# Long convolution and token MLP on one core: rows 0 and 1 of the last inverse step read four column blocks in place, with a new instruction order behind the last product

## The chip, the cores and the metric

The kernel runs on one core of one Trainium2 chip. The time is device microseconds of that core from launch to end. Each execution is one launch, and a time below is the median of several.

## The reference, cut to what matters

```python
# S = 2048 tokens, D = 448 channels, F = 1792
k_shift = sum(k_pad[:, t:t+S, :] * shift_k[:, 3-t] for t in range(4))     # short filter
kv = k_shift * v
y  = irfft(rfft(pad(kv, 2S)) * rfft(pad(ssm_k, 2S)))[:S]                  # long causal convolution
y  = y + kv * ssm_D
h  = x + layernorm(x) * y                                                 # x = A_q
u  = gelu(einsum("bsd,sf->bdf", layernorm(layernorm(h)), w1) + b1)        # MLP over tokens
h2 = h + transpose(einsum("bdf,fs->bds", u, w2) + b2)
```

## The kernel before, in words

The core has five queues: TensorE (PE in the profile), ScalarE (ACT), VectorE (DVE), GpSimd (POOL) and SyncE (SP, which only issues DMAs; POOL issues some too). One large SBUF tensor, "arena", holds everything, and PSUM has eight banks. The order of every queue is written out by hand in the table `ORDER`: a token `i2.1:0-3` means operations 0 to 3 of step 1 of stage `i2`. A small scheduler in the kernel reads this order, places the buffers and the semaphore waits; each engine then runs its list strictly in order.

The long convolution is done as matrix products with sine tables, two steps forward (`k1`, `u1`, then `k2`, `u2`) and two steps back (`i1`, `i2`). Tokens are numbered 16 q + r, so that "row r" (r = 0 to 15) is a tile of 128 tokens by 448 channels.

- Stage `i1` has eight products, jj = 0 to 7, and runs them in the order 0, 6, 3, 4, 5, 2, 1, 7. Their steps are `i1.1` (jj 0), `i1.14` (6), `i1.8` (3), `i1.10` (4), `i1.12` (5), `i1.6` (2), `i1.4` (1) and `i1.16` (7). For each, DVE multiplies the two transforms (L1161), PE applies the inverse table in two halves of eight matmuls (L1178), and ACT or DVE copies each half out of PSUM (the helper `evac`, L739 or L742) into `TU`. A product fills two column blocks of `TU`, j = 2 jj and 2 jj + 1.
- A block is then turned from "partitions are rows and frequencies" to "partitions are blocks and frequencies" by DMAs from `TU` into `TZ` (L1201; for the last product L1190). POOL issues most of the 196 KB ones, SP the small ones. Row r of `TZ` has a part from every block.
- Stage `i2` makes row r by two matmuls (L1300) of the table `ET` with row r of `TZ`. The row therefore waits for the DMAs of all blocks. For rows 0 and 1 (`NZ = 2`) the blocks 14 and 15 of the last product are left out of `TZ` (zeros are put there by two DMAs, L1119). Instead four more matmuls (L1308) multiply these blocks where they stand in `TU` with a table `EW` that is zero but for the partitions of that row. Four DMAs (L1128) copy the needed rows of `ET` into `EW`. The last product uses a rearranged inverse table, `ML`, so that rows 2 to 15 stand in its first 112 partitions and rows 0 and 1 in the last 16.
- `ct.0`, `ct.1` and `ct.2` are 24 transposes (L1109) that make the rest of `ET`. `warm` are 14 matmuls (L1211) whose result nobody reads; they keep PE busy at chosen places.
- After its matmuls a row is combined with x (DVE, L1338 for rows 0 to 3, L1327 for the others after a gate on ACT L1317 or DVE L1319). Its statistics are taken: bn_stats on DVE for rows 0 and 1 (L1344), a sum on DVE and a sum of squares on ACT (L1356) for the others, which go in pairs. POOL turns them into a scale (L1366, L1369, L1371, L1376, power at L1380). DVE normalises the row into `Q` (L1386). The steps of rows 0 to 8 are, on PE, `i2.1`/`i2.2` (row 0), `i2.9`/`i2.10` (row 1), `i2.17`, `i2.20`, `i2.28`, `i2.32`, `i2.41`, `i2.45` and `i2.54`.
- The MLP's first half keeps seven PSUM banks, one for each block of 128 hidden units, and adds row by row: `mlp.r` is seven matmuls with `Q[r]` (L1433). Only one bank is then left for the `i2` rows that follow, so these stand between the `mlp` steps. The second half of w1 (L1443) and w2 (L1454) come after it; they are PE work without a pause.
- Statistics of x itself (`q` steps: bn_stats L1237, aggregate L1239 on DVE, then add and power on POOL, L1245 and L1248) and the normalised rows 0 to 3 (`xn`, L1270 on ACT) run beside stages `i1` and `i2`.

The in-place matmuls of rows 0 and 1 follow the two of `TZ`:

```python
for h in range(2):                       # L1300
    matmul(bank, ET[:, 2*r+h, :], TZ[:, r, h, :], start=(h == 0), stop=(h == 1 and r >= NZ))
if r < NZ:
    for h in range(2):
        for jx in range(2):              # L1308, j = 14, 15
            matmul(bank, EW[:, 4*r+2*jx+h, :], TU[:, 14+jx, h, :], start=False, stop=(last))
```

Of the kernel before, what the change touches and what calls it, by code (L numbers as in the profile page):

```python
# [7 lines left out]
ALU = mybir.AluOpType  # L8
# [575 lines left out]
def _build(nc, A_q, A_k, A_v, A_shift_k, A_ssm_k, A_ssm_D, B_w1, B_b1, B_w2, B_b2, out):  # L584
# [5 lines left out]
    Bsz, S, D = A_q.shape  # L590
# [48 lines left out]
    with ctx:  # L639
# [48 lines left out]
        EW = view(o_EW, [4 * NZ, 128], f16)  # L688
        o_ML = o_EW + 1024 * NZ
# [414 lines left out]
        def emit_ct(late):  # L1104
# [10 lines left out]
            if not late:  # L1115
                sch.t0 = T_CT + 1.0
                for jx in range(2):
                    p0 = pz(R // 2 - 1, jx)
                    op("sp", lambda e, W, p0=p0: e.dma_start(  # L1119
                        TZ[p0:p0 + 29:4, 0:NZ].rearrange("p r c d -> p (r c d)"),  # L1120
                        EW[8 * jx:8 * jx + 8].rearrange("p a b -> p (a b)")[:, 0:NZ * D].bitcast(bf16)
                        .unsqueeze(1).broadcast_to([8, 2, NZ * D])),
                       r=[(o_EW, 1024 * NZ)], w=[(o_TZ, NZ * 2 * DB, "zpool")], dmab=8 * NZ * 2 * DB, keng=4, est=660.0)
                for r in range(NZ):
                    for jx in range(2):
                        p0 = pz(R // 2 - 1, jx)
                        q0 = 8 * (R - NZ) + r
                        op("sp", lambda e, W, r=r, jx=jx, p0=p0, q0=q0: e.dma_start(  # L1128
                            EW[q0:q0 + 7 * NZ + 1:NZ, 4 * r + 2 * jx:4 * r + 2 * jx + 2].rearrange("p a b -> p (a b)"),
                            ET[p0:p0 + 29:4, 2 * r:2 * r + 2].rearrange("p a b -> p (a b)")),  # L1130
                           r=[r_ET(r)], w=[(o_EW + 1024 * r + 512 * jx, 512)], dmab=8 * 512, keng=4, est=660.0)

        def emit_ew():
            sch.t0 = T_EW
            op("pool", lambda e, W: e.memset(EW, 0.0), w=[(o_EW, 1024 * NZ)], est=1100.0, safter=shuf["u"])
# [15 lines left out]
        def emit_products_i1():  # L1151
            for jj in range(R // 2):
# [20 lines left out]
                mt = (MA, MB, MN) if jj < R // 2 - 1 else ML  # L1173
                for h in range(2):
                    for t, (tab, xy) in enumerate(((mt[0], 0), (mt[2], 3), (mt[1], 1), (mt[1], 2))):
                        for par in range(2):
                            P = slice(64 * par, 64 * par + 64)
                            k = op("pe", lambda e, W, b=bs[h], m=ms[h], par=par, t=t, tab=tab, xy=xy, P=P: e.matmul(  # L1178
                                Pb(b, par), tab[P, :], MR(m.slots[0])[P, xy, :], start=(t == 0), stop=(t == 3)),
                               r=r_iv if jj < R // 2 - 1 else [(o_ML, 768)], br=[ms[h]], bw=[bs[h]], n=D, est=94.5, mode=3)  # L1180
                            i1_last.append(k)
                    evac(lambda jj=jj, h=h: TU[:, 2 * jj:2 * jj + 2, h, :], lambda b=bs[h]: Ppair(b),
                         [(o_TU + (4 * jj + h) * DB, DB), (o_TU + (4 * jj + 2 + h) * DB, DB)], bs[h], 2 * D)
                if jj == R // 2 - 1:
                    for h in range(2):
                        for par in range(2):
# [3 lines left out]
                            k = op("pool" if h and par == 0 else "sp", lambda e, W, j=j, h=h, p0=p0: e.dma_start(  # L1190
# [6 lines left out]
                for par in range(2):  # L1197
                    j = 2 * jj + par
                    p0 = 64 * (j & 1) + 32 * ((j >> 1) & 1) + (j >> 2)
                    for q_, a, b_, j0 in (("sp" if j == 3 else "pool", 0, 112, 0), ("pool" if jj == 2 else "sp", 112, 128, 14)):  # L1200
# [25 lines left out]
        def emit_q():  # L1226
# [4 lines left out]
            for g in range(8):  # L1231
# [9 lines left out]
                if g >= 2 and g % 2 == 0:  # L1241
                    continue
                r0, nr = (2 * g, 2) if g < 2 else (2 * g - 2, 4)
# [40 lines left out]
        def emit_i2():  # L1284
# [5 lines left out]
            for g, (r0, ng) in enumerate(GR):  # L1290
                oh = o_hst + 64 * g
                hs = view(oh, [16], f32)
                for i in range(ng):
# [4 lines left out]
                    tz = [(o_TZ + r * 2 * DB, 2 * DB)]  # L1298
                    for h in range(2):
                        k = op("pe", lambda e, W, b=b, r=r, h=h: e.matmul(  # L1300
                            Pb(b), ET[:, 2 * r + h, :], TZ[:, r, h, :], start=(h == 0), stop=(h == 1 and r >= NZ)),
                           r=[r_ET(r)] + tz, bw=[b], n=D, after=av[-1:] if r >= 8 and h == 0 else ())
                    if r < NZ:
                        sch.t0 += 0.2
                        for h in range(2):
                            for jx in range(2):
                                j = R - 2 + jx
                                k = op("pe", lambda e, W, b=b, r=r, h=h, j=j, jx=jx: e.matmul(  # L1308
                                    Pb(b), EW[:, 4 * r + 2 * jx + h, :], TU[:, j, h, :], start=False, stop=(h == 1 and jx == 1)),
                                   r=[(o_EW + 1024 * r + 512 * jx + 256 * h, 256), (o_TU + (2 * j + h) * DB, DB)], bw=[b], n=D, safter=(k,))  # L1310
# [41 lines left out]
                    else:  # L1352
# [4 lines left out]
                                                                             scale=1.0 / math.sqrt(D),  # L1357
# [5 lines left out]
                if ng == 2:  # L1363
# [6 lines left out]
                                                                   op=ALU.mult), r=[(oh + 16, 8)], w=[(oh + 24, 8)], est=290.0)  # L1370
                    op("pool", lambda e, W, hs=hs: e.tensor_tensor(out=hs[:, 8:10], in0=hs[:, 2:4], in1=hs[:, 6:8],  # L1371
# [145 lines left out]
```

## Time and profile before

| what | value |
|---|---|
| median of 3 runs | 173.05 us (172.36 to 174.24) |
| the profiled execution | 172.33 us, of which span 170.4 us |
| PE busy in the span | 161.8 us (95%), 1425 matmuls |
| DVE, ACT, POOL busy | 99.8, 92.3, 60.0 us |
| granted TensorE clock | 1.000 |
| last product of `i1` ends issuing on PE | 70.76 us |
| first MLP matmul (`mlp.0`) | 79.82 us |
| PE, DVE, ACT, POOL busy in the 9.06 us between | 8.28, 8.94, 8.20, 5.92 us |

The span is the time from the first to the last instruction; the profiled execution's own time is 1.9 us longer. A PE matmul of 448 columns is shown some 0.35 us long, but the next one starts 0.19 us after it: they overlap. Where the text counts PE work, it counts the distance between starts.

### The profile page before, as it was taken

The page shows a single profiled execution, that of the slowest core. Times are in us where ns is not written, and L with a number is a line of the kernel's source. Part 1 is how long each engine was busy: PE and PEld are TensorE (multiplying, and loading weights), DVE is VectorE, ACT ScalarE, POOL GpSimd, SP SyncE. Part 2 cuts the span into 40 slices and gives each one's busy share as a digit, 9 for nine tenths or more (in the row PEclk, how much of TensorE's full clock was granted, in tenths as well). Part 3 has the DMA queues.
Part 4 walks back from the last instruction along what each step waited for, and adds up shares of the span by engine and source line. Part 5 has one row for each costly group of instructions (what it writes and reads, how often), then busy time and mean ns, then how long its engine had stood idle before and what let it go on. Part 6 is the DMA issues. An engine that isn't in the chain of part 4 may idle for free.

```text
span 170.4 us, 3574 instructions
## 1 busy us (share of the span) xinstructions
PE 161.8 (95%) x1425; PEld 94.8 (56%) x1425; DVE 99.8 (59%) x188; ACT 92.3 (54%) x132; POOL 60.0 (35%) x154
## 2 busy tenths in 40 slices
PE   6989999889889999999999999999999999999993
PEld 2776745442334334553455555555567777777783
DVE  7998988859999999999969710000003223132232
ACT  3699588988999999979857518311210000000000
POOL 8345737581810686466887820000000000000000
PEclk9999999999999999999999999999999999999999
DMA  5999687584959766658999999950000111101111
GB/s 169 416 332 374 196 251 290 207 330 161 283 147 365 275 184 192 186 152 250 364 379 402 417 425 418 416 232 0 0 0 4 54 54 54 54 0 58 54 54 54
DMA packets 15612, 35.15 MB, mean 206 GB/s; under 512 B 3756, under 2 KB 9724, under 8 KB 15596
## 3 DMA queue, kind: packets, MB, share of 16 engines
q1 hardware_dynamic: 12540, 28.39, 45.6%
q0 software_dynamic: 2912, 6.45, 12.0%
q8 instruction: 11, 0.18, 0.4%
q10 hardware_dynamic: 144, 0.08, 0.2%
q14 instruction: 5, 0.04, 0.1%
HBM read 22.05 MB, written 1.84 MB: 140 GB/s over the span
## 4 chain that ended last, share of the span: by engine, by line
PE 57%; ACT 22%; DVE 11%; DMA 5%; POOL 2%; issue 1%; SPq 0%; DVEq 0%
PE ps L1454 25%; PE ps L1443 12%; PE ps L1433 12%; ACT arena L739 10%; ACT arena L1070 5%; DMA arena<-arena 5%; DVE arena L1161 5%; DVE arena L1237 4%; PE ps L1095 3%; ACT arena L848 2%; PE ps L1026 2%; PE ps L1300 2%; ACT arena L740 2%; POOL arena L1076 2%; ACT arena L1317 1%; PE ps L1060 1%
## 5 line engine op out<-in xcount | busy, mean ns | idle before, releaser
L1457 DVE SCALAR_TENSOR_TENSOR arena<-ps,arena 128x448 bf16<-128x448 f32 (+2 forms) x17 | 11.1, 656 | 57.7 <-PE ps L1454 57.6
L1454 PE MATMUL ps<-arena 128*128 128x448 bf16 (+2 forms) x238 | 42.7, 342 | 0.0
L1454 PEld LDWEIGHTS ps<-arena 128*128 128x128 bf16 x238 | 33.3, 145 | 9.5
L739 ACT CAST arena<-ps 128x896 bf16<-128x896 f32 x30 | 24.6, 1013 | 0.2 <-PE ps L1095 0.2
L1433 PE MATMUL ps<-arena 128*128 128x448 bf16 x112 | 22.5, 353 | 0.2 <-DVE arena L1376 0.2
L1070 ACT CAST arena<-ps 128x896 bf16<-128x896 f32 x24 | 20.5, 915 | 3.2 <-PE ps L1060 3.2
L1076 POOL DMA_DIRECT2D arena<-arena x32 | 17.6, 555 | 11.8 <-ACT arena L1070 9.8
L1443 PE MATMUL ps<-arena 128*128 128x448 bf16 x112 | 21.3, 352 | 0.0
L1423 ACT ACTIVATE arena<-ps,arena 128x448 bf16<-128x448 f32 x14 | 8.3, 635 | 19.1 <-PE ps L1443 14.6
L1095 PE MATMUL ps<-arena 128*64 128x448 bf16 x128 | 15.2, 359 | 2.3 <-ACT arena L739 0.8
L1161 DVE TENSOR_TENSOR arena<-arena 128x1792 bf16<-128x1792 bf16 x16 | 16.7, 1086 | 0.3 <-ACT arena L739 0.2
L1433 PEld LDWEIGHTS ps<-arena 128*128 128x128 bf16 x112 | 10.9, 98 | 10.7 <-DVE arena L1386 0.6
L1443 PEld LDWEIGHTS ps<-arena 128*128 128x128 bf16 x112 | 11.0, 98 | 10.2
L1060 PE MATMUL ps<-arena 128*32 128x448 bf16 x256 | 15.0, 355 | 0.8 <-DVE arena L1008 0.5
L1178 PE MATMUL ps<-arena 64*128 64x448 bf16 x128 | 14.5, 351 | 0.1
L1201 POOL DMA_DIRECT2D arena<-arena x15 | 8.8, 593 | 13.2 <-ACT arena L739 13.2
L1095 PEld LDWEIGHTS ps<-arena 128*64 128x64 f16 x128 | 5.8, 108 | 10.7 <-ACT arena L739 2.9
L1178 PEld LDWEIGHTS ps<-arena 64*128 64x128 f16 x128 | 6.1, 94 | 8.2 <-ACT arena L739 2.5
L1008 DVE TENSOR_TENSOR arena<-ps,arena 128x512 bf16<-128x512 f32 (+1 forms) x16 | 9.1, 618 | 2.0 <-PE ps L993 1.8
L739 ACT COPY arena<-ps 128x1024 bf16<-128x1024 bf16 (+1 forms) x8 | 8.0, 1064 | 3.1 <-PE ps L967 3.1
L1356 ACT ACTIVATE arena<-arena 128x448 bf16<-128x448 bf16 x14 | 8.0, 574 | 2.7 <-DVE arena L1327 2.6
L1060 PEld LDWEIGHTS ps<-arena 128*32 128x32 f16 x256 | 5.1, 95 | 7.6 <-DVE arena L1008 2.5
(97 smaller groups left out, 192.9 us busy)
## 6 DMA issues: line engine op xcount, KB each, us to landing
arena<-in_B_w_dram SPq DMA_DIRECT2D x8, 896.0 KB, 6.1
arena<-in_B_w_dram SPq DMA_DIRECT2D x2, 2048.0 KB, 17.2
arena<-arena POOLq DMA_DIRECT2D x32, 112.0 KB, 3.4
arena<-arena SPq DMA_DIRECT2D x16, 224.0 KB, 3.2
arena<-in_B_w_dram SPq DMA_DIRECT2D x2, 1536.0 KB, 19.4
arena<-arena POOLq DMA_DIRECT2D x13, 196.0 KB, 4.2
arena<-in_A_k_dram SPq DMA_DIRECT2D x4, 448.0 KB, 5.4
arena<-in_A_v_dram SPq DMA_DIRECT2D x4, 448.0 KB, 9.0
```

Of the source, the lines that this page charges most:

```text
L739: return e.copy(out=dst(), in_=src())
L1008: return e.tensor_tensor(out=v, in0=u.rearrange("p t (r d) -> p t r d", d=64), in1=v, op=ALU.mult)
L1060: op("pe", lambda e, W, b=b, r=r, q=q, x=x, c0=c0: e.matmul(PS[32 * q:32 * q + 32, b.slots[x], 0:D], E[:, 2 * r + x, c0:c0 + 32], src[:, r ...
L1070: return e.copy(out=dst, in_=Ppair(b)) if W == "act" else e.tensor_copy(out=dst, in_=Ppair(b))
L1076: shuf[tag].append(op(q_, lambda e, W, g=g, i=i, a=a, nu=nu, jh=jh: e.dma_start(T[a + i:a + i + 4 * nu - 3:4].rearrange("p (j k) c d -> p ...
L1095: op("pe", lambda e, W, b=bs[h], h=h, j=j, c=c, par=par: e.matmul(PS[64 * par:64 * par + 64, b.slots[c], 0:D], FW[:, 64 * c:64 * c + 64], ...
L1161: op("dve", lambda e, W, m=m, i=i: e.tensor_tensor(out=MR(m.slots[0]).rearrange("p (x y) d -> p x y d", x=2), in0=TU[:, i].unsqueeze(2).br ...
L1178: k = op("pe", lambda e, W, b=bs[h], m=ms[h], par=par, t=t, tab=tab, xy=xy, P=P: e.matmul(Pb(b, par), tab[P, :], MR(m.slots[0])[P, xy, :], ...
L1433: op("pe", lambda e, W, r=r, fc=fc, b=bs[fc]: e.matmul(Pb(b), W1A[:, r, 128 * fc:128 * fc + 128], Q[:, r, :], start=(r == 0), stop=(r == R ...
L1443: op("pe", lambda e, W, r=r, fc=fc, b=b: e.matmul(Pb(b), W1B[:, r, 128 * (fc - n0):128 * (fc - n0) + 128], Q[:, r, :], start=(r == 0), sto ...
L1454: op("pe", lambda e, W, r=r, fc=fc, b=b, d0=d0, d1=d1: e.matmul(Pb(b)[:, d0:d1], W2[fc // 7][:, fc % 7, r:S:R], G[:, fc, d0:d1], start=(fc ...
L1457: op("dve", lambda e, W, r=r, b=b, d0=d0, d1=d1: e.scalar_tensor_tensor(out=X[:, r, d0:d1], in0=Pb(b)[:, d0:d1], scalar=bm[:, r:r + 1], in ...
```

## The change

- Blocks 2 and 3 (product 1) are treated for rows 0 and 1 as blocks 14 and 15 were: product 1 uses the table `ML` too, zeros go to its places in `TZ`, a second half of `EW` gets copies of `ET`, and four more matmuls a row read `TU` in place. These come first, ahead of the two on `TZ` (`i2.1:0-3`, then `4-5`, then `i2.2:0-3`; the same in `i2.9` and `i2.10`). SP issues six more DMAs for it (`ct0.1:6-11`), put ahead of three small ones that were there.
- Product 1's rows go to `TZ` by two DMAs, one on POOL and one on SP, where there were four. Of the last product's four, POOL now issues two and SP two (one and three before).
- The last product's first half is copied out of PSUM by DVE (`i1.16:9`), the second by ACT; before, ACT copied both.
- The scale of a pair of rows: the POOL operation behind the subtraction (L1376) is now done ahead of it, on the squared mean; for x, rows 4 to 7 are handled as two pairs.
- The order behind the last product is new on all queues: `ct.0` goes between rows 0 and 1 and `ct.1` behind row 1, rows 2 to 8 come in the order 7, 2, 5, 3, 6, 4, 8, `mlp.0` and `mlp.1` stand next to each other, and two bn_stats on DVE (`q.7`) move behind the combination of row 7. PE's order up to the last product is unchanged, and so are the 14 `warm` matmuls.

The core of the diff (line numbers behind `ORDER` are one higher in the new kernel):

```diff
 "pe":
-  "i1.16:17 warm.10:0 warm.4:0 warm.7:0 warm.6:0 warm.0:0 ct.2:0-7 warm.12:0 warm.3:0 ct.0:0-7 ct.1:0-6 warm.2:0 i2.1:0-1 "
-  "i2.2:0-3 i2.9:0 ct.1:7 i2.9:1 i2.10:0-3 i2.28:0-1 i2.17:0-1 i2.45:0-1 i2.20:0-1 i2.41:0-1 i2.32:0-1 i2.54:0-1 mlp.0:6 ..."
+  "i1.16:17 warm.10:0 warm.4:0 warm.12:0 ct.2:0 warm.3:0 ct.2:1-7 i2.1:0-5 i2.2:0-3 ct.0:0-7 i2.9:0-5 i2.10:0-3 ct.1:0-7 "
+  "warm.0:0 warm.7:0 warm.6:0 i2.45:0-1 i2.17:0-1 i2.32:0-1 i2.20:0-1 i2.41:0 i2.28:0-1 i2.54:0-1 i2.41:1 warm.2:0 mlp.0:5 ..."
 "act":
-  "i1.16:18 i1.16:9 ct.2:8 ct.0:8 xn.4:0 ct.1:8 xn.5:0 i2.29:0 i2.46:0 ..."
+  "i1.16:18 ct.2:8 xn.4:0 ct.0:8 xn.5:0 ct.1:8 i2.46:0 i2.33:0 i2.19:0 i2.29:0 ..."
 "dve":
-  "i1.16:0 q.4:0 q.4:2-3 q.4:1 q.3:1-3 q.5:0 q.5:2-3 q.5:1 q.6:2 q.6:0-1 q.7:0 q.7:2 xn.3:1 i2.3:0 q.6:3 i2.4:0 i2.11:0 ..."
+  "i1.16:0 q.3:2 q.3:1 q.4:0 i1.16:9 q.3:3 q.5:2 q.5:0 q.4:1-2 xn.3:1 q.5:1 q.5:3 q.4:3 i2.3:0 q.6:0 q.6:2-3 q.6:1 i2.4:0 i2.11:0 ..."
 "pool":
-  "... i1.6:22 q.2:4 i1.16:21 q.2:5 xn.3:0 q.4:4-5 q.6:4-5 i2.7:0 i2.23:0-1 i2.15:0 i2.23:2 i2.24:0 i2.25:0 ..."
+  "... i1.6:22 q.2:4-5 i1.16:21 i1.16:19 xn.3:0 q.3:4-5 q.4:4-5 q.6:4-5 i2.7:0 i2.15:0 i2.23:0-2 i2.24:0 i2.25:0 ..."
 "sp":
-  "... ct0.1:5 ct0.1:2-4 i1.14:20 i1.1:20 i1.1:22 i1.4:20 i1.16:22 i1.16:20 i1.16:19 w1a.1:0 i1.12:22 i1.4:21 i1.4:19 w1a.2:0 ..."
+  "... ct0.1:5 ct0.1:2-4 ct0.1:6-11 i1.14:20 i1.1:20 i1.1:22 i1.4:19 i1.16:20 i1.16:22 w1a.1:0 i1.12:22 w1a.2:0 ..."
...
-        EW = view(o_EW, [4 * NZ, 128], f16)
+        EW = view(o_EW, [8 * NZ, 128], f16)
...
+                for jj_, e0 in ((R // 2 - 1, 0), (1, 4 * NZ)):      # zeros into TZ and ET -> EW, now for products 7 and 1
...
-                mt = (MA, MB, MN) if jj < R // 2 - 1 else ML
+                mt = ML if jj in (1, R // 2 - 1) else (MA, MB, MN)
...
-                            k = op("pool" if h and par == 0 else "sp", ...      # last product, TU -> TZ
+                            k = op("pool" if par == 0 else "sp", ...
...
+                    if jj == 1:
+                        shuf["zpool"] = op("sp" if par else "pool", lambda e, W, j=j, p0=p0: e.dma_start(
+                            TZ[p0:p0 + 29:4, NZ:R].rearrange("p r c d -> p r (c d)"),
+                            TU[0:8 * (R - NZ), j].rearrange("p c d -> p (c d)")), ...)
+                        continue
...
+                    def short(e0, j0):                              # four matmuls in place: EW[e0 + ...] x TU[j0 + jx]
...
+                    if r < NZ:
+                        k = short(4 * NZ, 2)
                     for h in range(2):
                         k = op("pe", ... ET[:, 2 * r + h, :], TZ[:, r, h, :], start=(h == 0 and r >= NZ), ...)
                     if r < NZ:
+                        k = short(0, R - 2)
...
+                    op("pool", ... hs[:, 6:8] = hs[:, 6:8] * (1.0 + EPS) - EPS * EPS)      # ahead of the subtraction
...
-                op("dve" if ng == 1 else "pool", ... var = var * (1.0 + EPS) + EPS * EPS)
+                if ng == 1: op("dve", ... the same)
```

More of the change, by code (lines that the diff above doesn't have):

```diff
@@ L687, in _build @@
         o_EW = o_I2 + 128
-        EW = view(o_EW, [4 * NZ, 128], f16)
-        o_ML = o_EW + 1024 * NZ
+        EW = view(o_EW, [8 * NZ, 128], f16)
+        o_ML = o_EW + 2048 * NZ
         ML = [view(o_ML + 256 * k, [128], f16) for k in range(3)]
@@ L1116, in emit_ct @@
                 sch.t0 = T_CT + 1.0
[L1117 to L1123, printed above, removed]
@@ L1124, in emit_ct @@
-                for r in range(NZ):
-                    for jx in range(2):
[L1126 to L1131, printed above, removed]
+                for jj_, e0 in ((R // 2 - 1, 0), (1, 4 * NZ)):
+                    for jx in range(2):
+                        p0 = pz(jj_, jx)
+                        op("sp", lambda e, W, p0=p0: e.dma_start(
+                            TZ[p0:p0 + 29:4, 0:NZ].rearrange("p r c d -> p (r c d)"),
+                            EW[8 * jx:8 * jx + 8].rearrange("p a b -> p (a b)")[:, 0:NZ * D].bitcast(bf16)
+                            .unsqueeze(1).broadcast_to([8, 2, NZ * D])),
+                           r=[(o_EW, 1024 * NZ)], w=[(o_TZ, NZ * 2 * DB, "zpool")], dmab=8 * NZ * 2 * DB, keng=4, est=660.0)
+                    for r in range(NZ):
+                        for jx in range(2):
+                            p0 = pz(jj_, jx)
+                            q0 = 8 * (R - NZ) + r
+                            op("sp", lambda e, W, r=r, jx=jx, p0=p0, q0=q0, e0=e0: e.dma_start(
+                                EW[q0:q0 + 7 * NZ + 1:NZ, e0 + 4 * r + 2 * jx:e0 + 4 * r + 2 * jx + 2].rearrange("p a b -> p (a b)"),
+                                ET[p0:p0 + 29:4, 2 * r:2 * r + 2].rearrange("p a b -> p (a b)")),
+                               r=[r_ET(r)], w=[(o_EW + 256 * e0 + 1024 * r + 512 * jx, 512)], dmab=8 * 512, keng=4, est=660.0)
@@ L1133, in emit_ew @@
         def emit_ew():
             sch.t0 = T_EW
-            op("pool", lambda e, W: e.memset(EW, 0.0), w=[(o_EW, 1024 * NZ)], est=1100.0, safter=shuf["u"])
+            op("pool", lambda e, W: e.memset(view(o_EW, [512 * NZ], f32), 0.0), w=[(o_EW, 2048 * NZ)], est=1100.0, safter=shuf["u"])
             m3 = view(o_BD + 256, [3, 128], f16)
@@ L1189, in emit_products_i1 @@
                             o_h = o_TU + (2 * j + h) * DB
-                            k = op("pool" if h and par == 0 else "sp", lambda e, W, j=j, h=h, p0=p0: e.dma_start(
+                            k = op("pool" if par == 0 else "sp", lambda e, W, j=j, h=h, p0=p0: e.dma_start(
                                 TZ[p0:p0 + 29:4, NZ:R, h, :], TU[0:8 * (R - NZ), j, h, :]),
@@ L1240, in emit_q @@
                        w=[(o_qst + 16 * r, 8)], n=6)
-                if g >= 2 and g % 2 == 0:
+                if g >= 4 and g % 2 == 0:
                     continue
-                r0, nr = (2 * g, 2) if g < 2 else (2 * g - 2, 4)
+                r0, nr = (2 * g, 2) if g < 4 else (2 * g - 2, 4)
                 rs = [(o_qst + 16 * (r0 + i), 16) for i in range(nr)]
@@ L1298, in emit_i2 @@
                     tz = [(o_TZ + r * 2 * DB, 2 * DB)]
+                    k = None
+                    def short(e0, j0):
+                        k = None
+                        for h in range(2):
+                            for jx in range(2):
+                                j = j0 + jx
+                                k = op("pe", lambda e, W, b=b, r=r, h=h, j=j, jx=jx, e0=e0: e.matmul(
+                                    Pb(b), EW[:, e0 + 4 * r + 2 * jx + h, :], TU[:, j, h, :], start=(e0 > 0 and h == 0 and jx == 0),
+                                    stop=(e0 == 0 and h == 1 and jx == 1)),
+                                   r=[(o_EW + 256 * e0 + 1024 * r + 512 * jx + 256 * h, 256), (o_TU + (2 * j + h) * DB, DB)], bw=[b],
+                                   n=D, safter=() if k is None and e0 else (i2_prev[0] if k is None else k,))
+                        return k
+                    if r < NZ:
+                        k = short(4 * NZ, 2)
                     for h in range(2):
                         k = op("pe", lambda e, W, b=b, r=r, h=h: e.matmul(
-                            Pb(b), ET[:, 2 * r + h, :], TZ[:, r, h, :], start=(h == 0), stop=(h == 1 and r >= NZ)),
-                           r=[r_ET(r)] + tz, bw=[b], n=D, after=av[-1:] if r >= 8 and h == 0 else ())
+                            Pb(b), ET[:, 2 * r + h, :], TZ[:, r, h, :], start=(h == 0 and r >= NZ), stop=(h == 1 and r >= NZ)),
+                           r=[r_ET(r)] + tz, bw=[b], n=D, after=av[-1:] if r >= 8 and h == 0 else (),
+                           safter=(k,) if r < NZ else ())
+                    i2_prev = [k]
                     if r < NZ:
                         sch.t0 += 0.2
[L1305 to L1310, printed above, removed]
+                        k = short(0, R - 2)
                     i2_last.append(k)
@@ L1356, in emit_i2 @@
                         op("act", lambda e, W, hs=hs, r=r, i=i: e.activation(out=JK, in_=X[:, r, :], func=ACT.Square,
-                                                                             scale=1.0 / math.sqrt(D),
+                                                                             scale=math.sqrt((1.0 + EPS) / D),
                                                                              accum_out=hs[:, 2 + i:3 + i]),
```

23 lines of the change are left out of this document (16 added, 7 removed), and 61 rows, old and new, of the table ORDER.

## The prediction

> **What bounds the kernel now.** I read the chain that ended last first. From 81.44 us on it is PE alone but for the last two DVE additions: whatever moves `mlp.0` moves the end, and nothing behind it has slack to give back.
>
> ```profile
> 81.44 0.55 PE ps L1300 x2
> ...
> 93.53 10.60 PE ps L1433 x56
> 104.13 21.18 PE ps L1443 x112
> 125.31 42.09 PE ps L1454 x231
> ```
>
> The columns are start, duration, engine and line. 231 matmuls in 42.09 us are 0.182 us each, 56 in 10.60 us are 0.189 us: PE runs back to back.
>
> So I read PE's own timeline between the last product (its last start is 70.48) and the MLP, for what PE does there and where it waits.
>
> ```profile
> 70.76 1.12 PE L1211 MATMUL ps<-arena 128*128 128x448 f16 x5
> 71.72 0.61 PE L1109 MATMUL ps<-arena 128*128 128x128 f16 x8
> 72.17 0.54 PE L1211 MATMUL ps<-arena 128*128 128x448 f16 x2
> 72.54 1.00 PE L1109 MATMUL ps<-arena 128*128 128x128 f16 x15
> 73.38 0.35 PE L1211 MATMUL ps<-arena 128*128 128x448 f16 x1
> 74.15 0.54 PE L1300 MATMUL ps<-arena 128*128 128x448 bf16 x2 [0.41 <-DMA arena<-arena]
> ...
> 76.47 2.43 PE L1300 MATMUL ps<-arena 128*128 128x448 bf16 x12
> 79.10 0.55 PE L1300 MATMUL ps<-arena 128*128 128x448 bf16 x2 [0.20 <-ACT arena L1317]
> 79.82 1.50 PE L1433 MATMUL ps<-arena 128*128 128x448 bf16 x7 [0.17 <-DVE arena L1376]
> 81.44 0.55 PE L1300 MATMUL ps<-arena 128*128 128x448 bf16 x2
> ```
>
> Start, duration, operation, count, and in brackets the idle time that the view shows. A matmul's row is 0.35 us long, but the next may start 0.19 us after it, so the issue time lost is larger than the bracket. From start to start: 73.38 to 74.15 is 0.77, less 0.19 is **0.58** (row 0 waits for `TZ`); 78.55 (the twelfth of the group at 76.47) to 79.10 gives **0.36** (row 8 waits for row 7's gate); 79.30 to 79.82 gives **0.33** (`mlp.0` waits for DVE's `Q[0]`); 80.97 to 81.44 gives **0.28** (row 9 waits for a bank). Together PE loses 1.55 us. The rest is work: 8 `warm` x 0.19, 24 transposes x 0.056 (8 in 0.45 us) and 26 row matmuls x 0.19 are 7.80 us, and with the first three waits 9.07, against 9.06 us from 70.76 to 79.82.
>
> Then the other engines in these stretches: columns are the stretch, its length, busy time and count of PE, PEld, DVE, ACT and POOL, granted clock, DMA share, GB/s.
>
> ```profile
> 65.00:70.76 5.76, 5.76 (x47) 2.39 (x44) 5.73 (x11) 5.76 (x9) 2.75 (x5) 1.00 0.71 198
> 70.76:79.82 9.06, 8.28 (x60) 4.39 (x58) 8.94 (x31) 8.20 (x13) 5.92 (x12) 1.00 0.63 183
> 79.82:88.00 8.18, 8.05 (x42) 4.04 (x43) 7.92 (x26) 6.60 (x17) 6.39 (x16) 1.00 1.04 357
> ```
>
> DVE is as full as PE (8.94 of 9.06, then 7.92 of 8.18). ACT has some room, POOL more.
>
> Last, the DMAs that row 0 waits for: POOL's issues, and how long single ones took to land (taken from narrow windows at 56, 68 and 70 us).
>
> ```profile
> 67.01 1.71 POOL L1201 DMA_DIRECT2D arena<-arena  x3 [1.48 <-ACT arena L739]
> 70.25 1.15 POOL L1201 DMA_DIRECT2D arena<-arena  x2 [1.53 <-ACT arena L739]
> ...
> arena<-arena POOLq DMA_DIRECT2D x1, 196.0 KB, 3.3
> ...
> arena<-arena POOLq DMA_DIRECT2D x1, 196.0 KB, 5.2
> ...
> arena<-arena POOLq DMA_DIRECT2D x1, 196.0 KB, 3.8
> ```
>
> Product 1's POOL block is issued at 70.25 and lands 3.8 us later, 74.05: PE starts row 0 0.1 us behind that. Product 2's second block is issued at 67.6 and lands after 5.2, at 72.8. The same 196 KB took 3.3 us early on: POOL's transfers queue up here.
>
> **The change part by part.** The sum is made against the profiled execution (172.33 us, span 170.4). It lies 0.72 us under the median of 173.05, so the result is carried over to the median as a difference.
>
> *Added matmuls.* Eight of 448 columns, 8 x 0.19 = **+1.52 us**, on the path, since PE is the path from here to the end. The 14 `warm` stay.
>
> *The wait for `TZ`.* Rows 0 and 1 now need product 2's DMAs, not product 1's. PE gets to its first `TZ` matmul after 71.15 (third `warm`) + 2 x 0.19 + 8 x 0.056 + 4 x 0.19 = 72.74; the data are there at 72.8, and PE starts 0.1 behind that. Wait 0.58 -> 0.15: **-0.43**.
>
> *The other three waits.* From 72.9 PE has, up to `mlp.0`: 16 row matmuls of rows 0 and 1, 16 transposes, 4 `warm`, 14 row matmuls, 34 x 0.19 + 0.9 = 7.36 us, so `mlp.0` comes at 80.2 to 80.3 against 79.82. By then its partners should be ready. Row 7 comes first, so row 8 has its gate early (-0.36). `mlp.0` and `mlp.1` stand together, so row 9 has 1.33 us longer for its bank (-0.28). `Q[0]`: row 0's sums reach PSUM near 74.15, not 75.46, and DVE combines it by 74.9, not 76.2. But DVE has first to do the moved copy (1.09, the row of the same copy at 47.22), and drops the two bn_stats of `q.7` (2 x 0.54) from in front of it; the sum of its work ahead of `Q[0]` is the same, and row 2 now reaches it 0.2 later. `Q[0]` is ready at 79.8 to 80.1, before PE asks (-0.33). All three: **-0.97**. So the 1.55 us of waits shrink to 0.15, and 1.52 us of matmuls stand in their place.
>
> *DVE's cover.* It hides because the deferred bn_stats fall behind row 7's combination. They then push `Q[4]` and `Q[5]` by 1.1 us less what was saved; PE comes to these only 0.1 to 0.2 us later. Bounds 0 and 1.3 us (1.09 + 0.2, nothing recovered); I take **+0.1**, because DVE also has a gap of 1.59 us at 87.7 in which a lag would end.
>
> *Six more DMAs on SP*, two of 28 KB and four of 4 KB. They first wait for the four copies into `EW`, issued 57.2 to 59.9, to land, since the zero DMAs read the same region. No landing is shown for these; POOL's are 2.8 at the least, so 62.7 to 63.3. Six issues at 0.66 to 0.8 (SP's rows) are 4.2 us: 67.5. Three small DMAs that stood at 59.94 to 62.05 follow, 2.1 us: 69.6. Product 1's SP DMA can go at 69.98 as before. 0.4 us of room; if it is used up, the last product's landings move (76.2 now, some 75.9 then), and rows 2 to 8 ask for them only at 77.4. In place matmuls need `EW` at 71.98; the last copy is issued by 67.5 and should land near 70.5. Cost on SP nothing. On the DMA engines: 72 KB more, and 84 KB moved from 60-62 to 67-70 us, ahead of product 2's landing. Lowest 0 (beside POOL's queue in idle engine time, share 0.71), highest 156 KB / 198 GB/s = 0.79. I take **+0.2**, nearer the low end: around 60 us, where four of these small DMAs were in flight, POOL's took 3.6 to 4.0 and the queue built up only later.
>
> *At nothing:* the copy moved off ACT (the last landing comes 0.3 earlier, not waited for); `EW` twice as large (a memset of 0.95 us at 46.4, with POOL idle for 9 us behind it and SP's first reader at 49.2); product 1 by `ML` (same matmuls); four DMAs turned into two (SP loses 1.3 us ahead of the weight loads, which no PE row waits for); two power calls of 0.74 in place of one of 1.04 on POOL (in a wait of 1.04 us); the scale moved ahead (0.2 to 0.5 us earlier for DVE's normalisation from row 2 on, where PE does not wait).
>
> Sum: +1.52 - 0.43 - 0.97 + 0.1 + 0.2 = **+0.42 us**, 172.75 on the profiled execution and 173.45 on the median: call it 173.4. The best this place can give is all waits gone, -0.03 us: PE is then full from 70.5 to the end.
>
> **The rivals.**
>
> *A: the DMAs crowd each other.* Everything hangs on product 2's landing (72.8), with 0.06 us to spare. Each microsecond later is one at the end. Price up to 0.79, less the 0.2 counted: 174.0. For it: landings already grew from 3.3 to 5.2 us. Against: share 0.71. The Trainium skill, DMA: Bandwidth & Descriptors, Queues, rings and completion order, says that each DMA engine takes turns between the queue rows packet by packet; by that rule SP's packets slip in between POOL's waiting ones and the whole 0.79 is paid. No row here shows SP and POOL in such a queue together.
>
> *B: DVE becomes the bound (slower).* It carries one more copy in the only 18 us where it is full. If the bn_stats behind row 7 find no gap, `Q[2]` to `Q[6]` come late one by one, and PE waits up to 1.3 us in all: 173.45 + 1.2 = 174.65. It decides as soon as `Q[2]` is ready later than 83.2, when PE gets to `mlp.2`. For it: 7.92 of 8.18 us busy. Against: the gap at 87.7.
>
> *C: the waits removed are longer in an ordinary execution.* The median is 0.72 above the profiled one. If that is product 1's DMA landing late, the change takes it away: 172.7. For it: it is the only DMA wait here. Against: the chain has DMA steps before 35 us too, which vary alike in both kernels.
>
> *D: nothing moves in practice*, because `ct.0` now behind row 0 holds ACT up and rows 4 to 7 come late. ACT would have to lose 1.4 us; 173.4 + the rest.
>
> **How the numbers follow.** Forecast 0.48, A 0.17, B 0.17, C 0.14, D 0.04. The three runs shown spread by -0.7 and +1.2 us about their median, and 1% (1.73 us) is about what a measurement of this kernel can tell from no change. Slower by over 1% (above 174.8): half of B, a third of A, and a tenth of the rest: 0.21. Faster by over 1% (below 171.3) would need 1.7 us where at most 0.03 are to be had, or C with luck: 0.06. Within 1%: 0.73. Range: from C less the runs' 0.7, 172.0, to B and a little more, 175.0.
>
> **What would show it.** Right: PE starts the first `TZ` matmul of row 0 at 72.8 to 73.1, `mlp.0` at 80.1 to 80.5 with no wait over 0.2 us ahead of it, and PE is without gaps to the end, with 1433 matmuls. A: that first matmul at 73.3 or later. B: waits on DVE in front of L1433's successor between 83 and 91 us. Wrong altogether: `mlp.0` before 79.5, or a PE gap over 0.5 us anywhere behind it, or a difference ahead of 70 us, where both kernels have one order.

## The result and the profile after

The change makes the kernel 0.7% slower: the median went from 172.88 to 174.19 us (21 runs each), the ratio is 1.0068, 95% interval 1.005 to 1.0086, that is +1.18 us. Here and below, runs over 1.5% above their kernel's fastest, which stand at a granted clock of 0.99 or less, count in the medians but not in the ratios. The forecast was +0.35 to +0.42.

The profiled execution after the change took 174.51 us, span 172.6. Its product phase ended 0.91 us later than before's (the last product's last start is at 71.39, not 70.48), although the order up to there is the same on PE. Of the 0.91, 0.87 is there at 14 us already. Other executions below, of either order, end this phase anywhere from 70.5 to 73.8, so this is no part of the change. So the two are compared from this start on: to the start of the last w2 matmul it is 97.11 us before (70.48 to 167.59) and 98.37 after (71.39 to 169.76). **The stretch behind the products is 1.26 us longer**, which accounts for the whole of the 1.18. This is called the tail below.

PE's timeline after (start, duration, line, count, idle time in brackets), from the first in-place matmuls to the MLP:

```profile
72.89 0.95 PE L1316 MATMUL ps<-arena 128*128 128x448 bf16 x4
73.86 0.55 PE L1325 MATMUL ps<-arena 128*128 128x448 bf16 x2
74.25 0.92 PE L1316 MATMUL ps<-arena 128*128 128x448 bf16 x4
...
77.79 0.73 PE L1221 MATMUL ps<-arena 128*128 128x448 f16 x3
79.38 2.81 PE L1325 MATMUL ps<-arena 128*128 128x448 bf16 x14 [0.86 <-DMA arena<-arena]
82.03 0.35 PE L1221 MATMUL ps<-arena 128*128 128x448 f16 x1
82.22 2.81 PE L1460 MATMUL ps<-arena 128*128 128x448 bf16 x14
```

The four in-place matmuls (L1316) are work; the first on `TZ` (L1325, row 0) comes at 73.86, with 0.19 us of issue time lost (product 2's second block lands at 73.81). Then PE runs through rows 0 and 1 and the transposes without a gap, issues its last `warm` (L1221) at 78.16 and stands until 79.38, where row 7 begins: 1.22 less 0.19 is **1.03 us lost**, released by a DMA. From there to the end there is no gap: the waits ahead of row 8, `mlp.0` and row 9 are gone. The sum closes: +1.52 of matmuls, -1.55 of old waits, +0.19 + 1.03 of new ones is +1.19, against 1.26 measured.

The same stretches as before, moved with the end of the products (columns as above: length, PE, PEld, DVE, ACT, POOL, clock, DMA share, GB/s):

```profile
65.00:71.67 6.67, 6.67 (x55) 2.77 (x52) 6.67 (x12) 6.67 (x10) 3.65 (x7) 1.00 0.80 196
71.67:82.22 10.55, 9.66 (x69) 5.24 (x67) 9.08 (x29) 7.92 (x12) 7.55 (x16) 1.00 0.50 145
82.22:90.40 8.18, 8.18 (x44) 4.09 (x44) 8.13 (x25) 6.16 (x17) 5.87 (x15) 1.00 1.04 365
```

DVE is no fuller in the middle stretch than it was and PE is full in the third, so DVE does not hold PE up. In the first the DMA share rose from 0.71 to 0.80 while the bytes stayed (198 to 196 GB/s): the same traffic takes more engine time. Who uses it stands in SP's timeline, where each row is a run of DMA issues:

```profile
58.05 2.69 SPq L1130 DMA_DIRECT2D arena<-arena  x4
63.72 1.47 SPq L1121 DMA_DIRECT2D arena<-arena  x2
65.23 5.01 SPq L1130 DMA_DIRECT2D arena<-arena  x4
70.28 2.30 SPq L1211 DMA_DIRECT2D arena<-arena  x3
72.63 0.68 SPq L1203 DMA_DIRECT2D arena<-arena  x1
73.35 1.39 SPq L1192 DMA_DIRECT2D arena<-arena  x2
```

The first row is the four old copies into `EW`, 0.67 us each. Then come the six new ones: two zero DMAs (L1121), and four copies that now take 1.25 us each on the mean. Behind them stand the three small ones, product 1's and the last product's two. Those two land 5.3 and 5.1 us after their issue, at 78.69 and 79.19; the last is what row 7 waits for. Before, this trip took 2.7 to 2.9 us, and product 1's DMA went ahead of the products' end (70.48), not behind it:

```profile
69.98 0.68 SPq L1201 DMA_DIRECT2D arena<-arena  x1
72.03 2.19 SPq L1190 DMA_DIRECT2D arena<-arena  x3
```

The DMA queues after, in the one microsecond from 67 (packets, MB, share of the 16 engines; the first is POOL's queue, the second SP's):

```profile
q0 software_dynamic: 75, 0.16, 54.8%
q1 hardware_dynamic: 18, 0.03, 48.2%
```

16 engines x 0.482 us / 18 is 0.43 us for one of SP's packets, and 0.12 for one of POOL's. The trace's record of single packets tells which of SP's are slow: the 32 of the two zero DMAs, 1792 bytes each, which move from 66.2 to 69.8 and take 0.50 us on the mean (0.07 at the least), 16.0 us of engine time together. The copies' packets, 512 bytes each, take 0.03 us, and those of 4 bytes 0.01. So the copies are slow to issue, but do not move slowly.

### The profile page after: what moved, and what is told of

It is laid out like the page before. It is cut to its first block, busy times and chain, and to the rows that moved or that the text cites. A ratio compares the mean times of both kernels' runs of the same rounds, so it can differ in the third digit from the quotient of the medians.

```text
span 172.6 us, 3594 instructions
## 1 busy us (share of the span) xinstructions
PE 163.5 (95%) x1433; PEld 95.6 (55%) x1433; DVE 100.2 (58%) x188; ACT 92.6 (54%) x132; POOL 60.6 (35%) x157
## 4 chain that ended last, share of the span: by engine, by line
PE 74%; DMA 10%; ACT 10%; SPq 1%; DVE 1%; issue 1%; POOL 0%; DVEq 0%
PE ps L1481 24%; PE ps L1460 12%; PE ps L1470 12%; ACT arena L740 6%; DMA arena<-arena 6%; PE ps L1180 5%; DMA arena<-in_A_ssm_k_dram 5%; PE ps L1096 5%; PE ps L1061 4%; PE ps L994 4%; PE ps L1325 3%; ACT arena L1071 2%; ACT arena L741 2%; PE ps L1221 1%; PE ps L968 1%; PE ps L1040 1%
## 5 line engine op out<-in xcount | busy, mean ns | idle before, releaser
L740 ACT CAST arena<-ps 128x896 bf16<-128x896 f32 x29 | 23.8, 1014 | 0.2 <-PE ps L1096 0.2
L1071 ACT CAST arena<-ps 128x896 bf16<-128x896 f32 x24 | 20.5, 915 | 3.8 <-PE ps L1061 3.8
L1077 POOL DMA_DIRECT2D arena<-arena x32 | 17.5, 553 | 13.2 <-ACT arena L1071 11.5
L1211 POOL DMA_DIRECT2D arena<-arena x14 | 8.2, 590 | 11.7 <-ACT arena L740 11.6
L1247 DVE BATCH_NORM_STATS2 arena<-arena 128x6 f32<-128x448 bf16 x16 | 9.4, 612 | 0.0
```

The costliest lines, as they stand in the source:

```text
L740: return e.copy(out=dst(), in_=src())
L1071: return e.copy(out=dst, in_=Ppair(b)) if W == "act" else e.tensor_copy(out=dst, in_=Ppair(b))
L1077: shuf[tag].append(op(q_, lambda e, W, g=g, i=i, a=a, nu=nu, jh=jh: e.dma_start(T[a + i:a + i + 4 * nu - 3:4].rearrange("p (j k) c d -> p ...
L1247: op("dve", lambda e, W, bs=bs, r=r: e.bn_stats(out=bs, in_=X[:, r, :]), r=[(o_X + r * DB, DB)], w=[(ob, 24)], n=D, kind="1x")
```

## The experiments

The last matmul's start less the last product's end ("tail") is given for the profiles that are compared by it, beside the ratio to the kernel before, which ran on the same chip. Operations are those of the `ORDER` table: in the new kernel `ct0.1:6-7` are the two added zero DMAs and `ct0.1:8-11` the four added copies.

**e1_sp_early: SP's added work moved out of the way.** The zero DMAs go behind the two old ones, near 50 us; the three small DMAs go behind the weight load `w1a.1`. Operations are renumbered, 0 to 3 are the zero DMAs.

```diff
 "sp":
-  "ct0.1:1 ct0.1:0 w1a.0:0 ... ct0.1:5 ct0.1:2-4 ct0.1:6-11 i1.14:20 i1.1:20 i1.1:22 i1.4:19 ... w1a.1:0 i1.12:22 w1a.2:0 ..."
+  "ct0.1:1 ct0.1:0 ct0.1:2-3 w1a.0:0 ... ct0.1:4-11 i1.4:19 ... w1a.1:0 i1.12:22 i1.14:20 i1.1:20 i1.1:22 w1a.2:0 ..."
```

> The changed kernel, with SP's queue eased: the two zero DMAs for product 1 are issued right behind the two of the last product (near 51 us, so they no longer wait for the EW copies to land), and the three small DMAs i1.14:20, i1.1:20, i1.1:22 go behind the first weight load. The mathematics is the same. Theory Q (SP's queue: the six added DMAs hold SP from 63.7 to 70.2 us, product 1's and the last product's DMAs are issued 1.7 us late and land at 79.2, PE waits 1.0 us ahead of row 7): SP issues product 1's DMA as soon as its copy is done, the wait ahead of row 7 falls under 0.2 us, the time falls by 0.9 to 1.1 us, to 1.000 to 1.002 of before. Rival M (the landing is late because SP's 196 KB and the new split of the last product's four DMAs are slow together, whatever goes ahead of them): the wait stays at 0.7 to 1.0 us, the ratio at 1.006. Rival W (it is the eight matmuls): ratio 1.006.

Measured: 173.54 us, ratio 1.0014 (0.9981 to 1.0047). The profile's products ended late (73.77), the tail is 97.13 us, before's length, and PE has no gap in it. So the whole loss is in SP's added DMAs and where they stand; the rest of the change costs as much as it saves.

**e2_before_six: the same six DMAs in the kernel before.** The zeros go once more to where the old two go; the copies go to a second half of `EW` that nobody reads.

```diff
+                for jx in range(2):   # zeros, as L1121 of the new kernel
+                    ... e.dma_start(TZ[p0:p0 + 29:4, 0:NZ], EW[8 * jx:8 * jx + 8] ...)
+                for r in range(NZ):   # copies ET -> second half of EW, as L1130
+                    ...
 "sp":
-  "... ct0.1:5 ct0.1:2-4 i1.14:20 ..."
+  "... ct0.1:5 ct0.1:2-4 ct0.1:6-11 i1.14:20 ..."
```

> The kernel before with six more SP DMAs of the same sizes at the same place of SP's queue (the two zero DMAs once more to the same place, four ET copies to a part of EW that nobody reads), and nothing else. Q: SP is held some 6 us here as well, product 1's SP block and the last product's DMAs are issued 1.5 to 2.5 us late, PE waits that much longer ahead of rows 0 or 2 to 8; 1.006 to 1.012 of before. M and W: nothing on PE's path changes, 0.999 to 1.002.

Measured: 175.08 us, ratio 1.0137 (1.0082 to 1.0192), tail 98.69. In its PE timeline row 0 now waits for a DMA:

```profile
76.50 0.55 PE L1315 MATMUL ps<-arena 128*128 128x448 bf16 x2 [2.07 <-DMA arena<-arena]
```

And in SP's timeline the four copies are slower still, 5.83 / 4 = 1.46 us each:

```profile
64.95 5.83 SPq L1143 DMA_DIRECT2D arena<-arena  x4
```

From start to start PE loses 2.23 us there, and 0.58 before: +1.65, with a tail 1.58 longer. What row 0 waits for is product 1's DMA on SP, which stands behind the six and the three small ones: it is issued at 72.98, 1.81 us behind the products' end (before, 0.50 ahead of it), and lands after 3.47 us (before, 3.57). So this landing is late by its issue alone. Six DMAs with 72 KB do this without any other part of the change.

**e3_no_mm: the eight added matmuls left out.** Rows 0 and 1 then lack product 1's two blocks.

```diff
 "pe":
-  "... i2.1:0-5 i2.2:0-3 ct.0:0-7 i2.9:0-5 i2.10:0-3 ..."
+  "... i2.1:0-1 i2.2:0-3 ct.0:0-7 i2.9:0-1 i2.10:0-3 ..."
-                    if r < NZ:
-                        k = short(4 * NZ, 2)
```

> The changed kernel without the eight added matmuls: product 1's part of rows 0 and 1 is left out, all DMAs and the order stay. W: PE has 1.52 us less to do, 0.997 to 0.999 of before. Q and M: PE gets to row 7 some 1.5 us earlier, but the landing it waits for stays, so the wait grows from 1.0 to some 2.5 us and the time falls by under 0.3 us: 1.004 to 1.007.

Measured: 174.48 us, ratio 1.0068 (1.0031 to 1.0106). 1.52 us of PE work are gone and the time is that of the changed kernel: behind the products the landings set the pace and the matmuls only fill the wait. The profile of this run is 1.2 us above the median and shows something else. In PE's timeline row 0 waits 2.33 us:

```profile
75.09 0.91 PE L1323 MATMUL ps<-arena 128*128 128x448 bf16 x2 [2.33 <-DMA arena<-arena]
```

A stretch behind it, with the columns as before:

```profile
76.00:79.00 3.00, 3.00 (x17) 1.80 (x16) 1.47 (x3) 0.62 (x1) 1.03 (x3) 0.63 0.28 84
```

The number behind the POOL column is the granted clock: after the long wait it is 0.63 from 76 to 79, and matmuls there come 0.37 us apart.

**e4_act_evac: the last product's first half copied out by ACT again.**

```diff
 "act":
-  "... i1.16:18 ct.2:8 ..."
+  "... i1.16:18 i1.16:9 ct.2:8 ..."
 "dve":
-  "... q.4:0 i1.16:9 q.3:3 ..."
+  "... q.4:0 q.3:3 ..."
```

> The changed kernel with the last product's first half copied out by ACT again, behind the second half; DVE loses that 1.05 us copy. Q: SP's queue is the limit, so the copy's end matters little: the last landing moves by 0 to 0.5 us, the ratio to before is 1.006 to 1.010. If instead DVE is what makes PE late (rival B of the prediction), the time falls by 0.5 us or more, to 1.003 or less.

Measured: 174.35 us, ratio 1.0079 (1.0045 to 1.0113). The profile's tail is 98.10, with DMA waits of 0.38 us at row 0 and 0.54 ahead of row 7. Not told apart from the change; the split of the copy is not where the time went.

**e7_small_behind: the three small DMAs moved, the six left in place.** SP then goes straight from the six to product 1's DMA; if SP's lateness were all, this would mend much of it.

```diff
 "sp":
-  "... ct0.1:6-11 i1.14:20 i1.1:20 i1.1:22 i1.4:19 i1.16:20 i1.16:22 w1a.1:0 i1.12:22 w1a.2:0 ..."
+  "... ct0.1:6-11 i1.4:19 i1.16:20 i1.16:22 w1a.1:0 i1.12:22 i1.14:20 i1.1:20 i1.1:22 w1a.2:0 ..."
```

> The changed kernel with one thing undone: the three small DMAs i1.14:20, i1.1:20, i1.1:22 go behind the first weight load, the six added ones stay as they are. If what hurts is only how late SP is: its 2.3 us for these three are saved, product 1's block goes out on time (SP free at 70.2, the copy ready near 70.9), the wait ahead of row 7 is under 0.3 us, ratio 1.000 to 1.003. If the six added DMAs also crowd the transfers behind them: product 1's and the last product's blocks still land late, a wait of 0.3 to 1.0 us, 1.003 to 1.007.

Measured: 175.31 us, ratio 1.0091 (1.0059 to 1.0123, from four runs): no better. The six run from 63.87 to 71.9 (6.27 us for the four copies). Product 1's DMA goes at 71.96 and the last product's at 72.85 and 73.59, 0.5 to 0.7 us earlier than in the changed kernel, and the last product's still land only at 78.65 and 79.15. Product 2's block, which POOL issues, now lands at 76.01, 7.5 us after its issue (5.3 in the change) and 4.65 us behind the products against 2.42, and PE loses 2.03 us there. So the wait in SP's line is not all: the transfers are slow too, POOL's among them. How much each is worth this run does not part, since product 1's DMA still goes 0.60 us behind the products' end. (This profile is 2 us above its median; its ratio carries the verdict.)

**e8_zeros_early: the zero DMAs alone moved.** The opposite half of e1: zeros near 50 us, the three small ones in front as in the change.

```diff
 "sp":
-  "ct0.1:1 ct0.1:0 w1a.0:0 ... ct0.1:5 ct0.1:2-4 ct0.1:6-11 i1.14:20 i1.1:20 i1.1:22 i1.4:19 ..."
+  "ct0.1:1 ct0.1:0 ct0.1:2-3 w1a.0:0 ... ct0.1:4-11 i1.14:20 i1.1:20 i1.1:22 i1.4:19 ..."
```

> The changed kernel with the other half of e1 alone: the two zero DMAs go out near 51 us, the four EW copies and the three small DMAs stay ahead of product 1's. In the changed kernel the four copies behind the zero DMAs took SP 1.25 us each, in e1 six in a row 0.66 each. If the zero DMAs are what blocks SP: the eight copies take 0.66 us each from 58 us on, 63.5, and the three small ones 2.1, so SP is free by 66, early enough; wait under 0.2 us, ratio 1.000 to 1.002. If it is the number of SP's DMAs that counts, SP is late again and the ratio is 1.004 to 1.007.

Measured: 173.10 us, ratio 1.000 (0.9976 to 1.0024), tail 97.12. SP's timeline:

```profile
49.43 3.07 SPq L1122 DMA_DIRECT2D arena<-arena  x4
...
58.19 5.37 SPq L1132 DMA_DIRECT2D arena<-arena  x8
63.60 2.47 SPq L1213 DMA_DIRECT2D arena<-arena  x3
71.03 0.68 SPq L1205 DMA_DIRECT2D arena<-arena  x1
73.02 1.39 SPq L1194 DMA_DIRECT2D arena<-arena  x2
```

All eight copies take 0.67 us each and are issued by 63.6, 6.7 us earlier than the change has its last; nothing waits for the zeros any more. The DMA queues from 67 to 68 us:

```profile
q0 software_dynamic: 92, 0.20, 74.9%
q1 hardware_dynamic: 23, 0.03, 8.2%
```

SP's 23 packets take 0.06 us each, not 0.43. The three small DMAs' packets, 1792 bytes like those of the zeros, move from 65.7 to 69.4, beside POOL's, and take 0.08 us each, not 0.50. In the four microseconds from 66 POOL's queue moves 0.78 MB here and 0.75 before, but 0.69 in the change and 0.65 in e2. Product 2's block lands 1.55 us behind the products, the last product's last DMA at 77.50, 0.8 us ahead of row 7. PE's timeline from there:

```profile
78.27 2.81 PE L1327 MATMUL ps<-arena 128*128 128x448 bf16 x14
80.92 0.35 PE L1223 MATMUL ps<-arena 128*128 128x448 f16 x1
81.10 2.81 PE L1462 MATMUL ps<-arena 128*128 128x448 bf16 x14
```

No bracket is left. The place of two DMAs of 28 KB, and with them of the four copies that follow, is the whole loss.

**e9_spread: the zero DMAs where the change has them, but read from spread partitions.** In the change the sources are partitions 0 to 7 and 8 to 15; here every eighth one.

```diff
-                            EW[8 * jx:8 * jx + 8].rearrange(...)
+                            EW[jx:jx + 57:8].rearrange(...)
```

> The changed kernel with one thing altered: the zero DMAs read their zeros from partitions 0, 8, 16 to 56 of EW (the second from 1, 9 to 57), not from partitions 0 to 7 and 8 to 15. Same bytes, same place in SP's queue, same waits. In the changed kernel 18 packets of SP's (25 KB) took 48% of the 16 engines' time between 67 and 68 us, 0.34 to 0.43 us a packet. Theory P (the packets are slow because all eight engines read the same eight partitions): they take 0.1 to 0.2 us, the EW copies behind them leave SP at 0.66 us each, product 2's second block lands at most 2.4 us behind the last product's matmuls, the wait ahead of row 7 falls under 0.3 us, ratio 0.999 to 1.002. Theory T (it is the time: two kinds of queue at once in the engines, wherever the zeros come from): packets as slow as before, ratio 1.005 to 1.009. The Trainium skill, Advanced Engine Details and Errata, DMA Bandwidth Details, says that each of 16 ports into the memory serves eight partitions at 27.2 GB/s; by that page P is the likelier.

Measured: 173.82 us, ratio 1.0065 (1.0041 to 1.0088), which says that the sources do not matter. The profile says that they do in part. Its DMA queues from 67 to 68:

```profile
q0 software_dynamic: 88, 0.13, 43.3%
q1 hardware_dynamic: 32, 0.04, 32.9%
```

In its SP timeline, the four added copies:

```profile
65.52 3.87 SPq L1130 DMA_DIRECT2D arena<-arena  x4
```

A packet of SP's takes 16 x 0.329 / 32 = 0.16 us, one of the zeros' own 0.20 on the mean (0.50 in the change), a copy's issue 0.97; row 7 loses 0.38 us and the tail is 97.50, so two thirds of the 1.26 are gone. One profile and six runs disagree, and this stays open. The Trainium skill, Advanced Engine Details and Errata, DMA Bandwidth Details, states that each SBUF port serves eight partitions alone. Whether the eight that a zero DMA of the change reads are one port's, that section does not say. The shorter packets speak for a crowd at the source, the ratio does not.

**Looking for a faster kernel: e5, e6, e10, e11.** With landings early, four `warm` matmuls (0.76 us) looked spare.

e5_less_warm is e1 and this:

```diff
-        N_WZ, N_WI, N_W0, N_WK, N_WJ = 14, 0, 9, 1, 0
+        N_WZ, N_WI, N_W0, N_WK, N_WJ = 10, 0, 9, 1, 0
 "pe":
-  "... ct.1:0-7 warm.0:0 warm.7:0 warm.6:0 i2.45:0-1 ... i2.41:1 warm.2:0 mlp.0:5 ..."
+  "... ct.1:0-7 i2.45:0-1 ... i2.41:1 mlp.0:5 ..."
```

> The kernel of e1_sp_early without the four warm matmuls behind row 1 (warm.0, 7, 6 and 2 of the new order; ten stay). In e1 PE has no gap behind the last product, so they cost 4 x 0.19 = 0.76 us unless something else is late. If PE alone is the bound now: 0.7 us less than e1, 0.997 to 0.998 of before. If DVE comes next (in e1 Q[0] was ready only 0.15 us before mlp.0): a wait of 0.5 to 0.6 us ahead of mlp.0 and a gain under 0.25 us, 0.999 to 1.001.

Measured: 173.14 us, ratio 1.0001 (0.9979 to 1.0023), tail 97.21. PE loses 0.43 us ahead of the first `TZ` matmul and 0.38 ahead of `mlp.0`, on `Q[0]` from DVE: 0.81 for 0.76 saved.

e6_less_warm_act is e5 with e4's edit.

> e5 with the last product's first half copied out by ACT again, which takes 1.05 us off DVE. If DVE is the next bound behind SP's queue: no wait on DVE ahead of mlp.0, 0.6 us less than e1, 0.996 to 0.998 of before, the fastest of all. If the last product's landing is next: the copy ends 0.8 us later, two of its DMAs land up to 0.8 us later, PE waits 0.2 to 0.9 us ahead of row 7, and nothing is gained over e5.

Measured: 173.7 us, ratio 1.0029 (0.9996 to 1.0061), tail 97.18. Both waits of e5 are all but gone and 0.64 us ahead of row 7 has come in their place. It ends 0.7 us behind the last landing (77.23), so it is no DMA. It ends 0.11 us behind DVE's combination of row 1 (to 77.86); the view names no releaser, so that DVE is what was late is argued.

e10_rows is e6 with e8's zeros and e9's sources in place of e1's order of the small DMAs, and rows 2 and 3 ahead of row 7; e11_rows_dve is the same with the copy on DVE.

```diff
-  "i2.45:0-1 i2.17:0-1 i2.32:0-1 i2.20:0-1 i2.41:0 ..."
+  "i2.17:0-1 i2.20:0-1 i2.45:0-1 i2.32:0-1 i2.41:0 ..."
```

> A version meant to beat both: e6_less_warm_act with the zero DMAs early and spread over partitions, and rows 2 and 3 ahead of row 7. In e6 PE waited 0.50 us ahead of row 7 while ACT still copied that row's part of ET; rows 2 and 3 need no such copy. If ACT's copy was the wait: no gap over 0.2 us up to mlp.0, mlp.0 9.1 us behind the last product's last matmul (9.34 before, 9.58 in e6), 0.997 to 0.999 of before. If DVE or the landing follows at once: a gap of 0.3 us or more elsewhere, ratio 1.000 to 1.002.

> e10_rows with the last product's first half copied by DVE, as in the changed kernel. If DVE is the bound ahead of mlp.0 (e5 waited 0.38 us there): the wait is there again, 0.3 to 0.6 us over e10, ratio 0.999 to 1.002. If not: as e10 or 0.1 us less.

Measured: 173.88 us, ratio 1.0067 (1.0047 to 1.0087), and 173.72, 1.0053 (1.0024 to 1.0082). Both miss. e10 loses 0.35 us at the first `TZ` matmul, 0.64 at row 2, again 0.11 behind DVE's combination of row 1, and 0.45 at `mlp.2`; so ACT's copy for row 7, which e10 meant to pass by, was hardly the wait in e6. e11 loses 0.16 at row 2, 0.19 at `mlp.0`'s first matmul, 0.44 at its fourth and 0.49 at `mlp.2`. Each wait taken out here has come back at another row. No kernel here beats the one before; e1, e5, e6 and e8 cannot be told from it.

## Why the prediction was right, and where it was not

The time lies within 1% of before and in the range, on the side that was forecast. The size did not hold: +0.4 forecast, +1.18 measured. The range, 172.0 to 175.0, had room for that error; the matmuls and the old waits were worked out rightly, the DMAs were not.

- **Added matmuls, +1.52.** Right: e8 and e1 have 1.52 us more PE work in a tail of before's length, because 1.55 us of waits went.
- **Wait for `TZ`, -0.43.** Measured 0.58 to 0.19, -0.39. Product 2's second block lands at 73.81, 2.42 us behind the products' end; the forecast had 72.8, which is 2.32.
- **The other three waits, -0.97.** All three are gone, as worked out.
- **DVE, +0.1, rival B.** No wait on DVE up to the end; B is refuted for this kernel. That DVE is next in line shows in e5.
- **"Cost on SP nothing" is the step that failed.** "Six issues at 0.66 to 0.8 ... are 4.2 us" were 6.5 (63.72 to 70.24), since the copies' issue rose to 1.25 us; against 0.4 us of room. Product 1's DMA went 1.24 us behind the products' end (72.63 - 71.39), in e8 0.50 ahead of it. The text had the consequence ready ("the last product's landings move") and thought them safe, some 75.9 for an asker at 77.4. PE was ready for row 7 at 78.35 on the later clock, 77.44 on before's, as forecast; the landing came at 79.19, or 78.28 on before's clock: 2.4 us late.
- **DMA crowding, +0.2 of 0 to 0.79, mis-sized.** It priced bytes, 156 KB at 198 GB/s. The 56 KB of the two zero DMAs alone took 16.0 us of engine time, which is 1.0 us of all 16 engines. With SP's lateness, which comes from the same DMAs, the loss is 1.03 us of issue time in the change and 1.65 in e2, where the upper bound was 0.79. The two are not parted. In e2 PE waits for a DMA that SP issued late, in e7 for a slow transfer of POOL's. In the change the last landing is 7.80 us behind the products' end against 5.94 in e8: 0.47 of it by the later issue, 1.39 by the longer trip. A part of that trip is a queue: its data start to move at 75.5, when product 1's DMA, itself late, is all but through (75.8).
- **Rival A** had the right mechanism and the wrong place. It looked at product 2's landing, which held in the change (it moved in e7); the loss fell on the last product's. The rule of the Trainium skill that it cites, on DMA engines taking turns between queues packet by packet, fits POOL's queue losing speed (0.69 MB in the four microseconds from 66, against 0.75 before) while SP's packets are among its own; it does not say why one of the zeros' takes 0.50 us.
- **Rival C** (an ordinary execution gains more) is refuted: the ratio of many runs and the tail of one profile give the same. **Rival D** is refuted too: behind the products PE waits for nothing but the two DMA landings.
- **What would show it.** The first `TZ` matmul was forecast at 72.8 to 73.1 and is at 73.86, 72.95 with the 0.91 of start-up taken off. `mlp.0` was forecast at 80.1 to 80.5 with no wait over 0.2 ahead of it; it is at 82.22, or 81.31, and the 1.03 ahead of row 7 is the difference. "A difference ahead of 70 us" was listed as wrong altogether; it is there, 0.91, but it is start-up: e10 and e11, with the changed order on PE, end the products at 70.63 and 70.52, and e2, with the old one, at 71.17.

Left open: why the zeros' packets take so long and why the copies behind them are slow to issue. That the place of the zero DMAs is what matters is shown (e8). POOL's full queue alone does not make such packets slow: e8's small DMAs have the same size beside it, at 0.08 us. The source alone does not either: the change's two old zero DMAs read the same 16 partitions near 50 us, when POOL's queue is empty, and take 0.25 us a packet at the most (an estimate: the weight load's packets of that size, not told apart from them, are taken at the least of 0.07). It takes both together, as far as single profiles tell; e9 says that the source has a part in it. How the two meet is not shown.

## What to carry to other kernels

A small DMA added to a queue that seems idle must be priced where it runs, not by its bytes: look at the packets of the other queues in that microsecond, and ask which landing is next behind it with the least room. When a step is worth "nothing", its cover has a size; here 1.5 us of room for the last product's landing was less than what 72 KB took. Where a transfer has no reason to be late, such as zeros into a buffer long free, issue it early: that alone was worth the whole loss.

## What the runs showed of the hardware

- An SP issue is not a fixed price: the same copy took 0.67 us at 58 us and, on the mean of four, 1.25 to 1.57 at 65 us, behind two zero DMAs (the change, e2, e7), and 0.67 for all eight when these were gone (e8).
- Two DMAs can take far more of the engines than their bytes: 32 packets of 1792 bytes took 0.50 us each in the change and 0.51 in e2, and 48 of the same size 0.08 in e8, in the same stretch of the kernel and beside the same queue of POOL's. Which partitions they read has a part in it (0.20 in the one profile of e9).
- A wait of PE can cost more than its length. In e3 PE stood idle for 2.33 us and in e7 for 1.87. The granted clock fell to 0.50 near the end of the first wait (74.80) and 0.65 us behind the second (76.71), for 3.41 us in both, with matmuls 0.37 us apart; in e2 it stood idle for 2.07 us and the matmuls behind it come 0.19 us apart. What tells these apart is open. The Trainium skill, TensorE: Matmul & The Clock Gate, What's actually happening, gives a free-running window of some 3.4 us and half the clock after an idle one; the half and the 3.41 us agree, but here no 3.4 us were without a matmul and the clock fell all the same, so the measurement is the stricter of the two. That the window is free-running could explain why e2 escaped; no run here shows it.
